# Four edits to the expert stage of an attention, expert and mixing kernel: no branch hints, other places for the half sums, other dealing of the decodes, an earlier turn in the last expert

## The chip, the cores and the metric

The kernel runs on one core of one Trainium2 chip. The metric is device time in microseconds (us) of one launch. Three runs of the kernel before took 632.85 to 635.07 us, with a median of 633.88 us. One further run was recorded by the profiler; it took 635.4 us, and every row below is from it.

A core has five engines that each work through an instruction list of their own: PE (matrix multiplication, with its weight loads shown apart as PEld), DVE (vector), ACT (scalar), POOL and SP. Here SP issues the large loads, and POOL issues gathers, scatters and some writes. Engines wait for each other and for transfers (DMA) by semaphores.

## The reference

Three parts follow each other. The middle one, a mixture of experts with one expert for each token, is the part that matters:

```python
x = attention(q, k, v)                  # 2 x 768 tokens of 512
for b, s in tokens:
    e = argmax(x[b, s] @ w_gate)        # or the expert of the token before, where a gate says so
    p = softmax(x[b, s] @ w_gate)
    h = maximum(x[b, s] @ w1[e], 0)     # 512 -> 1024
    out[b, s] = p[e] * (h @ w2[e])      # 1024 -> 512
# then: FFT over both axes, real part, add, normalise, feed-forward 512 -> 2048 -> 512
```

All operands are float32. The kernel keeps the precision by splitting each operand into a high part and a low rest (names ending in h and l, such as `sl0h` and `sl0l`), and it multiplies three times: high by high, high by low, low by high.

## The kernel before, in words

Attention comes first, with the routing of the tokens beside it. The experts 0 to 7 follow (here e0 to e7), from 118 to 318 us, and then the FFT and the feed-forward part up to 633 us.

The routing sorts tokens by expert into blocks of 128. `expert` (L1262) handles one expert. For experts 1 to 6 two versions of the code stand behind a branch on the number of blocks: `wide` for two blocks or more, `narrow` for one. Every engine takes this branch by itself (`L1348` in the profile is its line). With the data here, e4 and e6 are narrow and the others wide. The branch falls through into `wide`; `narrow` stands behind it in the instruction list. In the kernel before, a hint for PE's branch is given one expert ahead (its instruction has line L1936 in the trace).

The narrow version does this. `first128` (L1232) multiplies the 128 tokens by w1 in two halves `u` of 512 columns. PE forms a half in PSUM; ACT copies it to SBUF as a half sum, `hs[u]` (L1259); PE turns the half sum in four transposes (L1243); ACT applies the maximum and makes the high part `hh` (L1245); DVE makes the low part `hl` (L1246). The second half is turned later, inside `second` (L1197), which multiplies by w2 into `y` (L1204): after five of its 24 matmuls, `late()` issues the transposes of half sum 1. At the end ACT scales `y` into a tile named `ys` (L1186), and POOL scatters it to the output rows (L1191).

While PE works for expert e, ACT and DVE prepare the weights of expert e+1. This is the background, a list of steps that the foreground deals out: `step()` after every third matmul takes two steps, and `drain()` takes all that are left. A weight arrives in units of 1 MB in four raw buffers; SP's load for the unit four places on in a fixed order (`plan`, `shade` L958) is issued when a unit is finished. A unit `e` takes two casts on ACT (`take`, L1048) and two subtractions on DVE (L1050); a unit `d` is a decode for the feed-forward weights: one ACT pass into a tile `dec` (L1081), four DVE passes (L1090 to L1096), and a write of 512 KB by POOL's queue (L1014). Expert e has four `e` units, two in each half of its work, and up to two decodes. `tokens` (L1171) also runs in the background: it turns the next expert's tokens (`turn`, L1158: four transposes on PE, ACT makes `xh`, DVE makes `xl`) and issues the gathers of the expert after that into `xg0`, `xg1`, and a third one for block 2. `place(e, 2)` is that third gather buffer of expert e.

The tile name `dec` has two buffers, the name `ys` two as well. In the kernel before, a narrow expert's half sums stand in a `dec` tile.

The last expert, e7, takes `first128` and `second` for each of two blocks, and a third block (`third`, L1286) between them. `rest` (L1374) is a loop for more blocks that the data here doesn't need; it is a branch that is skipped.

Of the kernel before, what the change touches and what calls it, by code (L numbers as in the profile page):

```python
# [11 lines left out]
F32 = mybir.dt.float32  # L12
# [11 lines left out]
P = 128  # L24
B, H, S, D = 2, 8, 768, 64
E, F = 8, 1024
DM = H * D
# [643 lines left out]
SPLIT = 6  # L671
WARM = 6, 6, 3
TOKENS = 4
CASTS = (5, 6, 7, 8)
RESTS = (24, 25, 26, 27)
AHEAD = dict(enumerate([0, 1, 2, 2, 2, 1, 1, 1, 4, 0, 0, 0, 0, 0, 1, 0, 0, 4, 1, 1, 1, 0, 0, 0, 2, 1, 1, 1], 4))
# [260 lines left out]
class Ring:  # L937
# [20 lines left out]
    @staticmethod  # L958
    def shade():

        d = iter([("d", n) for n in range(2 * EARLY)])
        plan = []
        for e in range(E - 1):
            g = 4 * e + 4
            a = [("e", g), ("e", g + 1)]
            b = [("e", g + 2), ("e", g + 3)]

            for _ in range(-(-min(e + 1, E - 2) * 2 * EARLY // (E - 2)) + -min(e, E - 2) * 2 * EARLY // (E - 2)):
                (a if len(a) == 2 else b).append(next(d))
            plan.append((a, b))  # L970
        plan.append(([("t", 0), ("t", 1)], []))
        return plan
# [127 lines left out]
class Moe:  # L1100
# [158 lines left out]
            A.copy(hs[u], ps)  # L1259
        return lambda: turned(1)  # L1260

    def expert(self, e, n, more, ahead=None):  # L1262
        tc, ring = self.tc, self.st.ring
        pc, ent = self.pc[e % 2], self.ent[e % 4]
        w1, w2 = rows(self.st, 4 * e), rows(self.st, 4 * e + 2)
# [11 lines left out]
        def result(c, h, y, ys, *more):  # L1277
            y = self.second(*h, w2, *y, *more)
            bg.drain()
            last = e == LAST and c == 1  # L1280
            write = lambda: self.write(y, pc[:, c:c + 1], ent[:, c, 1:2], ys, "first" if last else None)
            if last:
                self.finish = write
            else:
                write()

        def third():
            self.weight(e, (2,))

            with tc.If(n > 2):  # L1290
                for _ in self.turn(2, 0, self.place(e, 2)):
                    pass
                if e == LAST:
                    self.rest(more)
                late = self.first128(w1, *self.more, spare, spare)
                result(2, self.more[1], spare, "more", lambda: None, late)

        def pieces():
            for units in ring.plan[e]:
# [23 lines left out]
                    result(at + 1, own(hs, 1), spare, "more")  # L1323

        def narrow():
            first, then = pieces()
            bg.add(chain(*first))
            h = own((self.hh[0], self.hl[0]), 0)
            late = self.first128(w1, own((self.xh[e % 2], self.xl[e % 2]), 0), h, (self.ps_h, "h"), (self.ps_x, "xtp"), step)
            bg.drain()  # L1330
            bg.add(chain(*then))
            calls = iter(range(8))

            def behind():
                if next(calls) == TOKENS:
                    bg.add(self.tokens(e + 1))
                bg.step(2)

            result(0, h, (self.ps_y, "y"), "ys", behind, late)

        if e < LAST:
            if e + 2 < E:
                self.entries(e + 2)
                tc.mark_branch_hint_location(f"wide{e + 1}", hint=(ahead > 1), engines=[mybir.EngineType.PE])
            if e == 0:
                wide()
                return
            with tc.If(n > 1, label=f"wide{e}") as arm:  # L1348
                wide()
            with arm.Else():  # L1350
                narrow()
            return

        for c in range(2):
            x, h = (own(s, c) for s in ((self.xh[e % 2], self.xl[e % 2]), (self.hh[0], self.hl[0])))
            late = self.first128(w1, x, h, (self.ps_h, "h"), (self.ps_x, "xtp"), step, [x[:, :DM] for x in self.xg[:2]])
            if c == 0:
                third()
                bg.add(chain(*first))
            result(c, h, (self.ps_y, "y"), "ys", step, late)  # L1360
            if c == 0:
                self.fetch(0)
# [56 lines left out]
    def run(self):  # L1419
        tc, st = self.tc, self.st  # L1420
        nc = tc.nc
        ring = st.ring
        self.entries(0, (1, 2))
        for x in self.xg[2:]:
            nc.vector.memset(x, 0.0)
        rows = self.gathers(0, (1, 2))
        self.entries(1)
        w = ring.load(2 * PIECES - 2)
        tc.add_manual_dep(w.ins, rows[1].ins.name, mybir.DependencyInfo(mybir.DependencyClass.Sync, mybir.DependencyReason.DATA),
                          reason="this load would hold the rows up")  # L1430
        self.scatter(st.ye, st.ent0[:, 1:2])
        spare = self.ps_more.tile([P, DM], F32, name="more")
        keep_busy(nc, st, spare, WARM[0])
        counts = nc.values_load(st.nch[0:1, E + 1:E + 2], min_val=0, max_val=2 * 4 ** E - 1)
        keep_busy(nc, st, spare, WARM[1])
        for _ in self.tokens(0):
            pass
        keep_busy(nc, st, spare, WARM[2])
        ring.load(2 * PIECES - 1, nc.scalar)
        for e in range(E):  # L1440
            self.expert(e, (counts >> 2 * e) & 3 if e < LAST else counts >> 2 * e, counts >> 2 * E, (counts >> 2 * (e + 1)) & 3 if e + 2 < E else None)


def post(tc, ctx, st):
# [495 lines left out]
```

## Time and profile before

| what | us |
|---|---|
| median of three runs | 633.88 |
| the profiled execution | 635.4 |
| span in it, first to last instruction | 633.6 |
| e2, e3, e5, wide | 23.4, 23.5, 23.6 |
| e4, narrow, 220.6 to 242.3 | 21.7 |
| e6, narrow, 265.9 to 282.4 | 16.5 |
| e7, 282.4 to 318.0 | 35.6 |

[...]

### The profile page before, as it was taken

Reading aid. Unit: us, or ns where it says so; the run is one execution under the profiler, and the core shown is the slowest. Engines: PE = TensorE matmul, PEld = TensorE weight load, DVE = VectorE, ACT = ScalarE, POOL = GpSimd, SP = SyncE. Lnnn points to the kernel's source line nnn. Section 1 sums busy time; section 2 is a strip of 40 time slices with the busy share of each in tenths; the row PEclk is TensorE's granted clock in tenths of the full one; section 3 lists DMA queues with packets and bytes.
Section 4 is the critical chain, followed back from the end, with each engine's and each line's share of the span. In section 5 each row is a group of like instructions: output and inputs, shape, how many; then the busy total and the mean of one; then the engine's idle time right before and its main releaser. Section 6 shows DMA issues by size and latency. Waiting matters only on the chain.

```text
span 633.6 us, 9722 instructions
## 1 busy us (share of the span) xinstructions
PE 609.5 (96%) x3506; PEld 494.1 (78%) x3507; DVE 383.8 (61%) x898; ACT 275.3 (43%) x548; POOL 100.5 (16%) x147
## 2 busy tenths in 40 slices
PE   9999998799999969898999999999999999999997
PEld 4777875499899849687867887888888888888885
DVE  5778786279786968661389987997531221272112
ACT  5789883266475556552434533441121221131010
POOL 2146662315313312300100000000000000000000
PEclk9999999999999989989999999999999999999999
DMA  8568762279978989961260242551100100100001
GB/s 278 187 204 203 201 120 68 49 283 337 372 250 278 335 288 327 339 210 66 87 250 32 95 173 92 187 190 63 67 0 1 32 36 0 67 2 0 1 0 66
DMA packets 25192, 92.49 MB, mean 146 GB/s; under 512 B 7645, under 2 KB 8797, under 8 KB 17185
## 3 DMA queue, kind: packets, MB, share of 16 engines
q1 hardware_dynamic: 19664, 79.50, 37.6%
q0 software_dynamic: 4736, 10.56, 4.6%
q10 hardware_dynamic: 720, 1.55, 0.7%
q8 instruction: 36, 0.59, 0.4%
q14 instruction: 36, 0.29, 0.2%
HBM read 81.00 MB, written 14.84 MB: 151 GB/s over the span
## 4 chain that ended last, share of the span: by engine, by line
PE 52%; DVE 1%; ACT 0%; issue 0%; DVEq 0%; ACTq 0%
PE h L1742 21%; PE acc L1757 7%; PE acc L1756 7%; PE acc L1758 7%; PE y L1204 1%; PE acc L1576 1%; PE acc L1562 1%; PE more L1254 1%; PE h L1254 1%; PE more L1204 1%; PE f L1708 1%; PE f L1605 1%; PE h L50 1%; PE f L1627 0%; DVE u L1767 0%; PE acc L1565 0%
## 5 line engine op out<-in xcount | busy, mean ns | idle before, releaser
L1747 DVE SCALAR_TENSOR_TENSOR hl<-h,hh 128x512 fp32r<-128x512 f32 x48 | 33.1, 689 | 117.5 <-ACT hh L1746 117.5
L1746 ACT ACTIVATE hh<-h 128x512 fp32r<-128x512 f32 x48 | 28.8, 600 | 164.3 <-PE h L1742 164.3
L1050 DVE TENSOR_TENSOR wide<-raws,wide 128x1024 fp32r<-128x1024 f32 (+1 forms) x38 | 44.8, 1201 | 24.4 <-ACT wide L1048 24.4
L168 ACT ACTIVATE t<-t,nm 128x256 f32<-128x256 f32 (+1 forms) x96 | 46.0, 480 | 10.7 <-DVE nm L159 9.9
L1742 PE MATMUL h<-un0h,wide 128*128 128x512 f32 (+1 forms) x136 | 42.4, 378 | 0.1
L1048 ACT CAST wide<-raws 128x1024 fp32r<-128x1024 f32 (+2 forms) x42 | 40.6, 993 | 4.1 <-PE acc L1758 3.4
L159 DVE CUSTOM_DVE_ANT_0 t<-sp,bias 128x256 f32<-128x256 f32 (+1 forms) x96 | 32.8, 398 | 8.3 <-PE sp L150 4.4
L1757 PE MATMUL acc<-wide,hh 128*128 128x512 f32 x96 | 37.8, 393 | 0.0
L1756 PE MATMUL acc<-wide,hh 128*128 128x512 f32 x96 | 37.6, 392 | 0.0
L1758 PE MATMUL acc<-wide,hl 128*128 128x512 f32 x96 | 37.5, 390 | 0.0
L1133 POOL DMA_INDIRECT xg<-xs,ent x23 | 28.7, 1250 | 39.9 <-PE y L1204 17.4
L1742 PEld LDWEIGHTS h<-un0h,wide 128*128 128x128 f32 x136 | 25.0, 188 | 5.0 <-ACT un0h L1517 0.3
L178 PE MATMUL tp<-consts,t 128*128 128x128 f32 x176 | 26.1, 283 | 1.7 <-ACT p L184 1.7
L178 PEld LDWEIGHTS tp<-consts,t 128*128 128x128 f32 x176 | 18.9, 141 | 9.3 <-ACT p L184 4.9
L1742 PE MATMUL h<-un0l,wide 128*128 128x512 f32 (+1 forms) x68 | 25.6, 377 | 0.0
L192 PE MATMUL sm<-p,vs 128*64 128x128 f32 x352 | 24.5, 279 | 0.0
L184 ACT COPY p<-tp 128x512 f32<-128x512 f32 (+1 forms) x48 | 24.3, 537 | 0.3 <-PE tp L178 0.3
L1081 ACT ACTIVATE dec<-raws 128x1024 f32<-128x1024 f32 x18 | 20.6, 1143 | 4.8 <-issue 4.8
L1224 PE MATMUL h<-xh,wide 128*128 128x256 f32 x160 | 22.5, 279 | 0.0
L1096 DVE SCALAR_TENSOR_TENSOR dec<-raws,dec 128x1024 int32<-128x1024 int32 x18 | 22.0, 1225 | 0.6
L1094 DVE SCALAR_TENSOR_TENSOR dec<-raws,dec 128x1024 int32<-128x1024 int32 x18 | 22.0, 1222 | 0.4
L192 PEld LDWEIGHTS sm<-p,vs 128*64 128x64 f32 x352 | 18.7, 136 | 3.8 <-issue 3.8
(474 smaller groups left out, 1602.3 us busy)
## 6 DMA issues: line engine op xcount, KB each, us to landing
raws<-we SPq DMA_DIRECT2D x31, 1024.0 KB
raws<-wm SPq DMA_DIRECT2D x18, 1024.0 KB
raws<-wmf SPq DMA_DIRECT2D x7, 1024.0 KB
wmf<-dec POOLq DMA_DIRECT2D x8, 512.0 KB
xs<-xrow SPq DMA_DIRECT2D x12, 260.0 KB
vs<-v SPq DMA_DIRECT2D x6, 512.0 KB
raws<-kq SPq DMA_DIRECT2D x3, 1024.0 KB
u<-x SPq DMA_DIRECT2D x6, 512.0 KB
```

Of the source, the lines that this page charges most:

```text
L159: V.tensor_tensor_reduce(out=u.t[:, x, :u.W], in0=u.sp[:, j, k, :u.W], in1=bias[:, 4 * u.g + x, u.b0:u.b0 + u.W], scale=-0.125, scalar=3.0 ...
L168: A.activation(u.t[:, x, :u.W], u.t[:, x, :u.W], AF.Exp, bias=u.nm[:, x:x + 1], scale=-1.0, accum_out=u.den[:, x])
L178: T.transpose(u.tp[k][:, j, c], u.t[:, 2 * k + j, c * P:(c + 1) * P], st.ident)
L192: T.matmul(turned[j * D:j * D + D, k], vs[:, ti % KS, u.h + 2 * k + j], u.p[:, 2 * k + j, c], start=c == 0, stop=c == len(tiles) - 1)
L1048: (first or nc.scalar.copy)(hi[:, cs], raw[:, cs])
L1050: (eng() if callable(eng) else eng or nc.vector).tensor_tensor(lo[:, cs], raw[:, cs], hi[:, cs].bitcast(F32), op=ALU.subtract)
L1742: nc.tensor.matmul(ps[:, c], a[:, k], x[:, k, c], start=n == 0, stop=n == 11)
L1746: nc.scalar.activation(hh, ps, AF.Relu)
L1747: nc.vector.scalar_tensor_tensor(hl, ps, 0.0, hh.bitcast(F32), op0=ALU.max, op1=ALU.subtract)
L1756: T.matmul(acc[c], hh[:, cs], h2, start=first, stop=False)
L1757: T.matmul(acc[c], hh[:, cs], l2, start=False, stop=False)
L1758: T.matmul(acc[c], hl[:, cs], h2, start=False, stop=last)
```

## The change

First, the number of decodes beside each expert is given by a tuple (`DECODED`) instead of a formula. The formula gives 2, 1, 1, 2, 1, 1, 0 for e0 to e6; the tuple 2, 1, 2, 2, 0, 1, 0. One decode moves from the first half of e4 to the second half of e2.

Second, the hints to PE's branches go, with the label and the argument that they need.

Third, in `narrow` all units of the expert go into the background in another order (the first two `e` units, then behind `drain` the other two and last the decodes), a step after three matmuls takes one unit of work instead of two, and the half sums stand elsewhere: the first in `place(e, 2)`, the second in a tile of the name `ys`.

Fourth, in the last expert the third block's tokens are turned in the background of the first block (always, not only if there is a third block), and `rest` follows the third block's result.

```diff
+DECODED = 2, 1, 2, 2, 0, 1, 0
...
-            for _ in range(-(-min(e + 1, E - 2) * 2 * EARLY // (E - 2)) + -min(e, E - 2) * 2 * EARLY // (E - 2)):
+            for _ in range(DECODED[e]):
                 (a if len(a) == 2 else b).append(next(d))
...
             with tc.If(n > 2):
-                for _ in self.turn(2, 0, self.place(e, 2)):
-                    pass
+                if e < LAST:
+                    for _ in self.turn(2, 0, self.place(e, 2)):
+                        pass
+                late = self.first128(w1, *self.more, spare, spare)
+                result(2, self.more[1], spare, "more", lambda: None, late)
                 if e == LAST:
                     self.rest(more)
-                late = self.first128(w1, *self.more, spare, spare)
-                result(2, self.more[1], spare, "more", lambda: None, late)
...
         def narrow():
-            first, then = pieces()
-            bg.add(chain(*first))
+            units = [u for part in ring.plan[e] for u in part]
...
+            takes = {u: ring.take(*u) for u in units}
+            d = [takes[u] for u in units if u[0] == "d"]
+            bg.add(chain(*(takes["e", 4 * e + 4 + k] for k in range(2))))
             h = own((self.hh[0], self.hl[0]), 0)
-            late = self.first128(w1, own((self.xh[e % 2], self.xl[e % 2]), 0), h, (self.ps_h, "h"), (self.ps_x, "xtp"), step)
+            late = self.first128(w1, own((self.xh[e % 2], self.xl[e % 2]), 0), h, (self.ps_h, "h"), (self.ps_x, "xtp"), bg.step,
+                                 [self.place(e, 2)[:, :DM], self.work.tile([P, DM], F32, name="ys", bufs=2)])
             bg.drain()
-            bg.add(chain(*then))
+            bg.add(chain(*(takes["e", 4 * e + 6 + k] for k in range(2)), *d))
...
-                bg.step(2)
+                bg.step()
...
-                tc.mark_branch_hint_location(f"wide{e + 1}", hint=(ahead > 1), engines=[mybir.EngineType.PE])
...
+        bg.add(self.turn(2, 0, self.place(e, 2)))
         for c in range(2):
```

On ACT, in the narrow version of e4, the list before is this; `dec` is the half sums' tile in the copies of L1259 and the decode's in L1081, `[waits ...]` names the semaphores (DMAHW are SP's loads, DMASW POOL's transfers).

```order
L1048 CAST wide_106<-raws_63 128x1024 [waits DVE_49]
L1259 COPY dec_8489<-h_8490 128x512 [waits DMASW0_49,DMASW1_49,DVE_49,PE_49]
L1081 ACTIVATE dec_8518<-raws_63 128x1024 [waits DMAHW3_49,DMASW5_49,DVE_49]
L1245 ACTIVATE hh256_6327<-xtp_8525 128x4x128 [waits PE_49]
L1259 COPY dec_8489<-h_8513 128x512 [waits PE_49]
L1048 CAST wide_106<-raws_63 128x1024 [waits DMAHW4_49]
L1245 ACTIVATE hh256_6327<-xtp_8551 128x4x128 [waits PE_49,Activation_49]
L1048 CAST wide_106<-raws_63 128x1024
```

The same place in the changed kernel has the decode no more, and the second half sum in a `ys` tile:

```order
L1260 COPY xg2_6353<-h_8463 128x512 [waits DMASW3_49,PE_49]
L1049 CAST wide_106<-raws_63 128x1024 [waits DMAHW3_49]
L1246 ACTIVATE hh256_6327<-xtp_8490 128x4x128 [waits DVE_49,PE_49,Activation_49]
L1049 CAST wide_106<-raws_63 128x1024
L1260 COPY ys_8462<-h_8481 128x512 [waits DMASW6_49,DMASW7_49,PE_49,Activation_49]
L1049 CAST wide_106<-raws_63 128x1024
L1246 ACTIVATE hh256_6327<-xtp_8515 128x4x128 [waits DVE_49,PE_49]
L1049 CAST wide_106<-raws_63 128x1024
```

The decode of L1081 stood ahead of both `hh` passes and waited for DMASW5, a transfer of POOL; now the second half sum's copy waits for two transfers of POOL, DMASW6 and DMASW7, behind the first `hh` pass.

Which transfers these are is seen on POOL in e3, the expert ahead, here in the changed kernel; the numbers behind a name tell one buffer's use from another.

```order
L1015 DMA wmf_99<-dec_7939 128x1024 [waits DMASW6_49,DVE_49]
L1192 DMA x2_101<-ys_7956,ent3_6335 1536x512 [waits DMASW7_49,Activation_49]
```

POOL issues a decode's write and right behind it the scatter of e3's first block, from a `ys` tile; with two buffers under that name, e4's half sum has the buffer that this scatter reads. The kernel before has the same two instructions in the same order at this place.

On PE, in e7, the third block's turn into the PSUM tile `more` stood behind the branch (L1290) and right ahead of its matmuls:

```order
L1254 MATMUL h_9546<-sl5h_6318,xl1_6349 128x512 x2
L1290 REGISTER_ALU
L1290 COMPARE_AND_BRANCH
L1164 MATMUL more_9579<-consts_66,xg3_6354 128x128 [waits DMASW3_49]
L1164 MATMUL more_9579<-consts_66,xg3_6354 128x128 x3
L1395 REGISTER_ALU
L1395 COMPARE_AND_BRANCH
```

Now it stands three matmuls into the first block:

```order
L1355 UNCONDITIONAL_BRANCH
L1255 MATMUL h_9490<-wide_106,xh1_6346 128x512 [waits PE_49,Activation_49]
L1255 MATMUL h_9490<-wide_106,xh1_6346 128x512 x2
L1165 MATMUL more_9494<-consts_66,xg3_6354 128x128 [waits DMASW3_49]
L1165 MATMUL more_9494<-consts_66,xg3_6354 128x128 x3
L1255 MATMUL h_9490<-wide_106,xh1_6346 128x512
L1255 MATMUL h_9490<-sl5h_6318,xh1_6346 128x512
```

The turn moved ahead of 21 matmuls of the first block, and the branch of `rest` (L1395) behind the third block.

## Rows read from the trace of the kernel before

**Rows 1.** The page's first line

```profile
span 633.6 us, 9722 instructions
```

**Rows 2.** Stretches e2, e3, e4, e6, e7: busy us per engine, PE's clock, DMA share, GB/s

```profile
173.70:197.10 23.40, 23.25 (x153) 21.04 (x152) 16.87 (x21) 13.46 (x17) 5.95 (x7) 1.00 0.83 285
197.10:220.60 23.50, 23.35 (x154) 21.09 (x154) 20.41 (x25) 14.54 (x18) 6.21 (x6) 1.00 0.81 287
220.60:242.30 21.70, 16.24 (x66) 12.57 (x65) 15.14 (x17) 12.70 (x16) 3.75 (x4) 0.84 0.83 294
265.90:282.40 16.50, 14.48 (x64) 11.83 (x65) 10.40 (x10) 11.75 (x15) 1.00 (x1) 0.90 0.63 218
282.40:318.00 35.60, 34.00 (x162) 27.65 (x161) 10.34 (x18) 12.74 (x20) 2.94 (x3) 1.00 0.31 114
```

**Rows 3.** PE's waits, 118 to 330 us: total us, times, longest

```profile
PE y L1204 <- ACT hh L1245: 4.3, 1, 4.3
PE h L1254 <- ACT wide L1048: 2.0, 1, 2.0
PE more L1254 <- DVEq L1395: 1.6, 1, 1.6
```

**Rows 4.** Timeline of e4: start, us, engine, line, operation, [idle before <-releaser]

```profile
221.12 0.59 POOL L1014 DMA_DIRECT2D wmf<-dec  x1 [0.68 <-DVE dec L1096]
...
222.01 1.03 POOL L1191 DMA_INDIRECT x<-ys,ent  x1 [0.30 <-issue]
...
225.47 0.58 ACT L1259 COPY dec<-h 128x512 f32<-128x512 f32 x1
226.10 0.66 PE L1243 MATMUL xtp<-consts,dec 128*128 128x128 f32 x4 [1.16 <-ACT dec L1259]
...
230.80 1.12 ACT L1081 ACTIVATE dec<-raws 128x1024 f32<-128x1024 f32 x1 [4.75 <-issue]
231.81 0.59 ACT L1245 ACTIVATE hh<-xtp 128x512 fp32r<-128x512 f32 x1
232.45 0.79 PE L1204 MATMUL y<-sl0h,hh 128*128 128x512 f32 x1 [4.30 <-ACT hh L1245]
232.75 1.07 ACT L1048 CAST wide<-raws 128x1024 fp32r<-128x1024 f32 x1
233.28 0.68 DVE L1246 SCALAR_TENSOR_TENSOR hl<-xtp,hh 128x512 fp32r<-128x512 f32 x1
234.75 1.05 PE L1243 MATMUL xtp<-consts,dec 128*128 128x128 f32 x4
236.27 1.22 DVE L1050 TENSOR_TENSOR wide<-raws,wide 128x1024 fp32r<-128x1024 f32 x1
```

**Rows 5.** Shorter stretches, columns as in rows 2

```profile
222.00:232.00 10.00, 4.99 (x23) 3.48 (x21) 4.69 (x5) 5.25 (x7) 2.58 (x2) 0.99 0.98 354
...
232.40:238.60 6.20, 6.15 (x17) 4.88 (x18) 6.13 (x8) 4.12 (x6) 0.58 (x1) 0.50 0.46 136
...
267.90:272.80 4.90, 4.88 (x15) 3.86 (x16) 4.63 (x4) 3.36 (x4) 0.05 (x1) 0.65 0.79 254
```

**Rows 6.** PE's branches into e4 (216 to 220 us): ns min/median/max, first and last start

```profile
L1348 PEldq COMPARE_BRANCH  x2: 196/272/349, 216.5 to 217.3; - x2
```

**Rows 7.** The same into e6, 261 to 263 us

```profile
L1348 PEldq COMPARE_BRANCH  x2: 302/2913/5524, 261.7 to 262.2; - x2
```

**Rows 8.** PE's hints, all six

```profile
L1936 PEldq BRANCH_PREFETCH_HINT  x6: 32/36/39, 126.2 to 239.4; - x6
```

**Rows 9.** Timeline: PE's first matmul of e6

```profile
267.92 0.47 PE L1254 MATMUL h<-sl0h,xh 128*128 128x512 f32 x1 [2.03 <-ACT wide L1048]
```

**Rows 10.** Timeline of the third block's start in e7

```profile
288.47 0.60 PE L1164 MATMUL more<-consts,xg 128*128 128x128 f32 x4
...
289.78 0.69 DVE L1168 TENSOR_TENSOR xl<-more,xh 128x512 fp32r<-128x512 f32 x1 [1.07 <-ACTq L1395]
...
290.67 1.16 PE L1254 MATMUL more<-wide,xh 128*128 128x512 f32 x4 [1.60 <-DVEq L1395]
```

More of the change, by code (lines that the diff above doesn't have):

```diff
@@ L1260, in first128, with expert @@
         return lambda: turned(1)
-    def expert(self, e, n, more, ahead=None):
+    def expert(self, e, n, more):
         tc, ring = self.tc, self.st.ring
@@ L1325, in narrow @@
         def narrow():
-            first, then = pieces()
-            bg.add(chain(*first))
+            units = [u for part in ring.plan[e] for u in part]
+            for u in units:
+                if u[0] == "d":
+                    ring.begun.pop(ring.at[u], None)
+            takes = {u: ring.take(*u) for u in units}
+            d = [takes[u] for u in units if u[0] == "d"]
+            bg.add(chain(*(takes["e", 4 * e + 4 + k] for k in range(2))))
             h = own((self.hh[0], self.hl[0]), 0)
-            late = self.first128(w1, own((self.xh[e % 2], self.xl[e % 2]), 0), h, (self.ps_h, "h"), (self.ps_x, "xtp"), step)
+            late = self.first128(w1, own((self.xh[e % 2], self.xl[e % 2]), 0), h, (self.ps_h, "h"), (self.ps_x, "xtp"), bg.step,
+                                 [self.place(e, 2)[:, :DM], self.work.tile([P, DM], F32, name="ys", bufs=2)])
             bg.drain()
-            bg.add(chain(*then))
+            bg.add(chain(*(takes["e", 4 * e + 6 + k] for k in range(2)), *d))
             calls = iter(range(8))
@@ L1347, in expert @@
                 return
-            with tc.If(n > 1, label=f"wide{e}") as arm:
+            with tc.If(n > 1) as arm:
                 wide()
@@ L1440, in run @@
         for e in range(E):
-            self.expert(e, (counts >> 2 * e) & 3 if e < LAST else counts >> 2 * e, counts >> 2 * E, (counts >> 2 * (e + 1)) & 3 if e + 2 < E else None)
+            self.expert(e, (counts >> 2 * e) & 3 if e < LAST else counts >> 2 * e, counts >> 2 * E)
 def post(tc, ctx, st):
```

## The prediction

> **What bounds the kernel.** I read the page's first line, then the table by stretches, then the list of PE's waits, and last the timeline at each wait. PE sets the time nearly everywhere: in e2 and e3 it is busy for all but 0.15 us of 23.4 and 23.5 us [rows 2]. So an edit pays only where PE stands still, or runs at the lower clock. Between 118 and 330 us three waits are long: 4.3 us ahead of `y` in e4, 2.0 us ahead of e6, 1.6 us in e7's third block [rows 3]. e4 has 16.24 us of work in 21.7 us, at a mean clock of 0.84; e6 14.48 in 16.5, e7 34.00 in 35.6 [rows 2]. The change touches all three places.
>
> The timeline tells why e4 waits. POOL issued e3's decode write at 221.12 and a scatter behind it at 222.01. The decode of ACT (L1081), whose `dec` buffer that write reads, began at 230.80 after 4.75 us of idling put down to "issue", that is, to nothing that the profile shows. Behind it on ACT stood the first `hh` (231.81), and `y` could start only at 232.45 [rows 4]. So I take it that 512 KB took about 9.7 us to leave, in a stretch in which the DMA engines were 0.98 busy [rows 5]. After this, PE had the clock at 0.50 until 238.6 [rows 5].
>
> **e4, the decode goes.** Without it the first `hh` follows its transposes at once, and the 4.3 us wait as it is now vanishes. What is late next is the second half sum. Its copy stands in a `ys` tile and waits for two transfers of POOL; the order shows that they are e3's decode write and the scatter behind it, which reads the same buffer. Their landing has no row. The write's end is bounded by the decode's start, 230.80; the scatter was issued 0.89 us later (222.01 less 221.12), so it lands between 230.8 and 231.7, and I take 231.2, in the middle. The cover of the old wait is gone only in part: a wait on the same queue comes back, one half sum later, but with the first half of the work done before it.
>
> From there the chain is worked out. The copy takes 0.58, so it ends at 231.8. The next on ACT is a cast of 1.07, to 232.9. DVE then has four subtractions of the 1.22 kind, one `hl` of 0.68 and two `xl` of 0.69 [rows 4, 10]: 4.88 + 0.68 + 1.38 = 6.94, to 239.8. e5 uses its `xl` only after eight of its matmuls, about 1.0 us: e2's 23.25 us hold 96 matmuls of 256 columns and 48 of twice the width [rows 2], so a narrow one takes 23.25 / 192 = 0.12. So e5 starts as if at 238.8. PE's own chain is shorter: from the late transposes at 234.75 to e5 at 242.30 it took 7.55 us, 3.85 of it at half clock [rows 2, 4, 5], so about 5.6 at the full clock and 7.5 at worst, which gives 237.4 to 239.4 from 231.8. I take 238.7. Against 242.3 [rows 2] that is a gain of 3.6 us. With the landing 2 us later it is 1.6; with no wait on it at all, what PE, ACT and DVE have to do is left, and the gain is about 5.5.
>
> **e4, no hint.** The trace holds six hints and both outcomes: the branch into e4 took 0.349 us, the one into e6 5.524 us [rows 6, 7], and both had a hint about one expert earlier [rows 8]. Without one I cost e4's branch like e6's: between 0.35 and 5.52, and I take 5.52. It starts at 217.3 [rows 6], so PE enters e4 at 222.8 instead of 220.6, 2.2 us late. 24 matmuls of 0.24 follow and four transposes of 0.66 [rows 4], 6.4 us at full clock, to 229.2, and five of `y` to 230.4; the wait of 1.16 for the first half sum's copy at 225.47 [rows 4] may go or stay, since fewer casts are ahead of it. That is ahead of the half sum at 231.8, so the landing hides the stall. If the clock falls as it did behind e6's stall (0.65 of full over 4.9 us, a loss of 1.7 us [rows 5]), PE is there at 232.1, about level. So the term is 0 here; uncovered it is 2.2 to 3.9 us.
>
> [...]
>
> **e6.** Its wait of 2.03 us is put down to ACT's cast [rows 9], but the sequencer's branch of 5.524 us from 262.2 ends at 267.7, and PE starts at 267.92 [rows 7, 9]; I take the branch for the cause. A hint that did nothing there is removed, so the stall stays, and so do the 1.7 us of clock [rows 5]. The background now goes at half the pace, one step instead of two, and what is left comes behind `drain`; ACT is busy 11.75 of 16.5 us and DVE 10.40 [rows 2], so there is room. One side is a loss of 3.3 us, a second such wait inside e6's code, of which PE's queue covers a little less than of the first (5.52 less 2.03, 3.5 us); the other a gain of 1, should casts no longer stand ahead of `hh`. I take a loss of 0.5 for a cast of 1.07 that now stands between a half sum and its `hh` about half of the time.
>
> **e7.** The third block's turn was issued at 288.47, its `xl` at 289.78, and the matmuls that need it began at 290.67 after 1.60 us [rows 10]. Now the turn stands among the first block's matmuls, some 5 us earlier, and its ACT and DVE passes lie beside those. The four transposes of 0.60 stay on PE. The gather was long in place, since the turn at 288.47 waited for none. Late next would be the branch of `rest`, but it is now behind the third block, where PE has queued matmuls. Gain 1.6, bounds 0 and 1.7.
>
> **e2.** A second decode costs ACT 1.12 us [rows 4] and DVE about 3.5, the difference between e3, which has two already (20.41), and e2 with one (16.87); and e3 has no PE wait [rows 2]. The transfer grows by 1.5 MB, about 3.9 us at the 390 GB/s or so that e3's and e4's busiest stretches come to (354 in [rows 5], at a share of 0.98, would make it 4.2). e2 has 0.17 of 23.4 us free, 4.0 us [rows 2]. That just fits; if not, e3's weights come late and PE waits. Bounds 0 and 1.5 us; I take 0.2, near e3's row. Nothing is won there.
>
> **Sum.** 3.6 + 1.6 - 0.5 - 0.2 = 4.5 us. The profiled execution took 635.4 us, 1.8 beyond its span [rows 1], so 630.9; it lies 1.5 above the median of 633.88, and on the median this is 629.4 us. The FFT and the feed-forward part are PE-bound, and I cost them at nothing.
>
> **Rivals.** (A) The forecast, 627.6 to 631.2 us, chance 0.53.
>
> (B) A far branch without hint is not covered: a stall of 2.2 us and its 1.7 us of clock in e4, or the second such wait of 3.3 us in e6. For it: the e6 row, and new places of the code. Against: the landing at 231.2 covers e4. It takes 3.3 from the gain: 632.7. Chance 0.15: one branch in two stalls, but e4's is covered. [...]
>
> (C) e2's extra 1.5 MB doesn't fit, and e3's casts are late by 2 us: 631.4. For it: 3.9 against 4.0 us free. Against: e3 has two decodes at a share of 0.81. Chance 0.11.
>
> (D) The half sum's copy isn't held, since the scatter lands by 229: the e4 term is 5.5 instead of 3.6, which gives 627.5. For it: one transfer fewer is queued in e4. Against: the decode of before did wait until 230.80 [rows 4]. Chance 0.09.
>
> (E) Slower. The scatter behind e3's decode write lands much later, since with no decode in e4 its loads follow each other closer and take the DMA engines from POOL's queue, which were 0.98 busy already [rows 5]. ACT then stands at the half sum's copy, with every cast and `hh` of e4 behind it, and PE waits. Each us beyond 231.2 costs one: nothing is left at 231.2 + 4.5 = 235.7, and from 237.6 the kernel is slower by over 1.9. With a landing at 238 the time is 636.2. Against: the loads in flight are four of 1 MB in either kernel. Chance 0.12.
>
> **Numbers.** What a measurement here can tell from no change is about 0.3%, 1.9 us, so faster is below 632.0 and slower above 635.8. Faster: A, C, D but for their upper tails, 0.71. Same: B and these tails, 0.17. Slower: E, 0.12. The range leaves out most of E and half of the far tails: 627.0 to 633.0 us; its upper end holds B.
>
> **What would show it.** In the profile after, PE's wait ahead of the late transposes (L1244) in e4 should be named, 1 to 2 us, with ACT's half sum copy ending near 231.8 and idle ahead of it; e5's first matmul near 238.7; a branch of about 5.5 us into e4 and into e6; the third block's matmuls in e7 without a wait; e2 and e3 of 23.4 to 23.6 us. A copy that ends past 236, a second branch wait inside e6, or PE waiting in e3 for a cast would make the prediction wrong.

## The result, and the profile after

The changed kernel is slower: 639.73 us in the median of 20 runs against 635.26 us of the kernel before, ratio 1.0077 (95% interval 1.0061 to 1.0094). The forecast was 629.4 us and faster. It was worked out from a median of 633.88 us for the kernel before, so 1.4 of the 10.3 us between forecast and measurement are in that starting point. The profiled execution has a span of 638.2 us against 633.6 [rows 1].

The stages are measured from PE's first matmul of one expert to the first of the next, so a wait ahead of an expert counts for the one before it. The table holds the kernels that the text argues with; times are us.

| kernel | e0 | e3 | e4 | e5 | e6 | e7 |
|---|---|---|---|---|---|---|
| before | 23.1 | 23.4 | 21.7 | 25.6 | 14.5 | 38.6 |
| changed | 24.5 | 27.8 | 15.5 | 25.9 | 18.9 | 37.6 |
| changed, second profile (`again`) | 23.2 | 31.7 | 14.7 | 25.8 | 18.1 | 37.5 |
| dealing alone (`only1`) | 23.2 | 23.4 | 14.3 | 26.2 | 14.5 | 38.6 |
| dealing, decodes last in `narrow` (`dlast`) | 23.2 | 25.5 | 20.5 | 26.1 | 14.5 | 38.6 |
| changed, units in the plan's order (`inplan`) | 23.1 | 25.5 | 14.5 | 26.1 | 18.5 | 37.5 |
| changed, code moved (`pad`) | 23.2 | 28.0 | 14.3 | 28.3 | 14.5 | 37.5 |
| dealing and last expert, code moved (`only14s`) | 23.1 | 25.0 | 13.0 | 24.1 | 14.3 | 37.7 |

e4 gained 6.2 us and e7 1.0; e3 lost 4.4 and e6 4.4. In this execution e0 also began 1.4 us later than in the kernel before and took 1.3 us more; the run `again` below shows that these two belong to the one execution. PE's waits in the changed kernel, from 118 to 330 us (total us, times, longest), name the places; they answer to [rows 3]:

```profile
PE h L1255 <- issue: 5.7, 2, 3.7
...
PE h L1225 <- DVE hl L1229: 1.9, 1, 1.9
...
PE h L1255 <- ACT more L1187: 1.2, 1, 1.2
PE xtp L1244 <- ACT ys L1260: 1.0, 1, 1.0
PE xtp L1244 <- ACT xg L1260: 0.9, 1, 0.9
...
PE y L1205 <- PEq L1403: 0.6, 1, 0.6
```

The 4.3 us of e4 and the 1.6 us of e7 are gone, as forecast. New are 1.9 us in e3 for `hl`, and 5.7 us "issue" ahead of the narrow code: 2.0 at e4 and 3.7 inside e6. The stretches e2, e3, e4, e6 and e7 (columns as in [rows 2], the bounds being first matmuls):

```profile
176.40:199.82 23.42, 23.27 (x154) 21.06 (x153) 20.11 (x25) 14.49 (x18) 5.89 (x6) 1.00 0.80 276
199.82:227.63 27.81, 23.78 (x153) 21.04 (x152) 21.05 (x26) 15.10 (x19) 8.48 (x10) 1.00 0.90 323
227.63:243.09 15.46, 13.56 (x65) 10.32 (x65) 9.82 (x10) 10.90 (x14) 1.98 (x2) 1.00 0.85 291
...
269.01:287.89 18.88, 15.19 (x64) 12.19 (x65) 9.76 (x10) 10.68 (x14) 0.86 (x1) 0.82 0.51 167
287.89:325.48 37.59, 36.80 (x173) 29.52 (x171) 13.40 (x26) 13.58 (x23) 3.03 (x3) 1.00 0.38 138
```

e2 with its second decode is as long as before, at a DMA share of 0.80. The trouble begins in e3. Its timeline in the changed kernel (ACT, DVE, PE):

```profile
200.06 0.69 ACT L1187 ACTIVATE more<-more,pc 128x512 f32<-128x512 f32 x1 [4.80 <-PE more L1205]
...
204.53 1.05 ACT L1049 CAST wide<-raws 128x1024 fp32r<-128x1024 f32 x1 [3.77 <-DMA raws<-wm]
...
205.48 0.59 ACT L1228 ACTIVATE hh<-h 128x512 fp32r<-128x512 f32 x1
...
206.75 0.68 DVE L1229 SCALAR_TENSOR_TENSOR hl<-h,hh 128x512 fp32r<-128x512 f32 x1
...
207.49 0.39 PE L1225 MATMUL h<-xh,sl0h 128*128 128x256 f32 x1 [1.91 <-DVE hl L1229]
```

ACT stands 3.77 us at a cast of an expert's unit, and what releases it is a load of `wm`, the feed-forward weights, which this cast doesn't read. Behind it on ACT stands `hh`, behind that on DVE `hl`, and PE waits 1.91 us. The same in e4 (ACT and PE):

```profile
230.45 2.00 ACT L1049 CAST wide<-raws 128x1024 fp32r<-128x1024 f32 x2 [4.01 <-DMA raws<-we]
...
232.35 0.58 ACT L1260 COPY xg<-h 128x512 f32<-128x512 f32 x1
...
232.98 0.66 PE L1244 MATMUL xtp<-consts,xg 128*128 128x128 f32 x4 [0.92 <-ACT xg L1260]
...
236.52 0.59 ACT L1260 COPY ys<-h 128x512 f32<-128x512 f32 x1 [1.21 <-DMA wmf<-dec]
...
237.16 0.66 PE L1244 MATMUL xtp<-consts,ys 128*128 128x128 f32 x4 [0.98 <-ACT ys L1260]
```

Here the first casts wait 4.01 us with the first half sum's copy behind them. The last two rows are the wait that the prediction had named: the `ys` copy, for e3's decode write.

PE's branches into e4 and into e6 in the changed kernel (ns min/median/max, first and last start):

```profile
L1355 PEldq COMPARE_BRANCH  x2: 174/2884/5594, 221.4 to 221.9; - x2
```

```profile
L1355 PEldq COMPARE_BRANCH  x2: 281/2496/4712, 263.6 to 264.1; - x2
```

The first is 5.594 us where [rows 6] has 0.349. And e6 stops a second time, three matmuls and four weight loads in (PE's timeline):

```profile
269.01 0.47 PE L1255 MATMUL h<-sl0h,xh 128*128 128x512 f32 x1 [1.20 <-ACT more L1187]
269.32 0.39 PE L1255 MATMUL h<-sl0l,xh 128*128 128x512 f32 x1
269.55 0.40 PE L1255 MATMUL h<-sl0h,xh 128*128 128x512 f32 x1
273.64 0.58 PE L1255 MATMUL h<-sl0l,xh 128*128 128x512 f32 x1 [3.69 <-issue]
```

What PE's sequencer waits for is in the trace too. The view of DMA transfers has queues of the kind "instruction"; one of them, q8, moves packets of 16 KB (0.02 MB). In the straight code from 329.4 to 597.9 us of the kernel before it moved ten of them while PE ran 1255 matmuls and 1254 weight loads, 251 recorded instructions a packet. Within the branch into e4, from 221.9 to 227.5 us:

```profile
q8 instruction: 1, 0.02, 1.0%
```

The second stop of e6, from 269.9 to 273.6 us, holds one too; the branch of [rows 6] holds none. In the sixteen profiles of this text, all 23 branches into e4 and e6 that took 4.5 us or more hold such a packet, the nine of about 0.35 us hold none, and the sequencer goes on 1.3 to 1.5 us after the packet has ended. Behind a slow branch, then, and in the second stop, PE waits for instructions.

PE ran at the lower clock from 271.4 to 278.2 us, granted 0.50 of full speed, twice as long as behind the one stall ahead of e6 before (0.65 over 4.9 us is 3.4 us at half [rows 5]).

### The profile page after: what moved, and what is told of

It is laid out like the page before. It is cut to its first block, busy times and chain, and to the rows that moved or that the text cites. A ratio compares the mean times of both kernels' runs of the same rounds, so it can differ in the third digit from the quotient of the medians.

```text
span 638.2 us, 9698 instructions
## 1 busy us (share of the span) xinstructions
PE 609.3 (95%) x3506; PEld 493.5 (77%) x3507; DVE 383.6 (60%) x898; ACT 275.0 (43%) x548; POOL 101.1 (16%) x147
## 3 DMA queue, kind: packets, MB, share of 16 engines
q1 hardware_dynamic: 19664, 79.50, 37.6%
## 4 chain that ended last, share of the span: by engine, by line
PE 50%; DVE 1%; ACT 0%; issue 0%; DVEq 0%; ACTq 0%
PE h L1750 21%; PE acc L1765 7%; PE acc L1764 7%; PE acc L1766 7%; PE y L1205 1%; PE acc L1584 1%; PE acc L1570 1%; PE h L1255 1%; PE f L1716 1%; PE f L1613 1%; PE h L50 1%; PE f L1635 0%; DVE u L1775 0%; PE acc L1573 0%; PE f L1616 0%; PE acc L1635 0%
## 5 line engine op out<-in xcount | busy, mean ns | idle before, releaser
L1764 PE MATMUL acc<-wide,hh 128*128 128x512 f32 x96 | 37.6, 392 | 0.0
L1766 PE MATMUL acc<-wide,hl 128*128 128x512 f32 x96 | 37.5, 390 | 0.0
L178 PE MATMUL tp<-consts,t 128*128 128x128 f32 x176 | 26.1, 283 | 1.7 <-ACT p L184 1.2
L178 PEld LDWEIGHTS tp<-consts,t 128*128 128x128 f32 x176 | 18.9, 140 | 9.3 <-ACT p L184 4.2
L1750 PE MATMUL h<-un0l,wide 128*128 128x512 f32 (+1 forms) x68 | 25.6, 377 | 0.0
L192 PE MATMUL sm<-p,vs 128*64 128x128 f32 x352 | 24.5, 280 | 0.0
L1750 PE MATMUL h<-un1h,wide 128*128 128x512 f32 x64 | 21.3, 396 | 0.0
```

The source lines that it names most:

```text
L178: T.transpose(u.tp[k][:, j, c], u.t[:, 2 * k + j, c * P:(c + 1) * P], st.ident)
L192: T.matmul(turned[j * D:j * D + D, k], vs[:, ti % KS, u.h + 2 * k + j], u.p[:, 2 * k + j, c], start=c == 0, stop=c == len(tiles) - 1)
L1750: nc.tensor.matmul(ps[:, c], a[:, k], x[:, k, c], start=n == 0, stop=n == 11)
L1764: T.matmul(acc[c], hh[:, cs], h2, start=first, stop=False)
L1766: T.matmul(acc[c], hl[:, cs], h2, start=False, stop=last)
```

## The experiments

The medians of the kernel before lie between 633.0 and 635.3 us in the separate jobs, so each run is given by its ratio to the kernel before in the same job. Two kernels are compared by their ratios. Code is said to move by places: one place is one entry of PE's instruction list, and the matmuls used for it take two each, one for the weight load and one for the matmul.

**Code moved by matmuls that never run (`pad`).** In the arm for general attention, which this data doesn't take:

```diff
     with arm.Else():
+        with tc.tile_pool(name="ps_pad", bufs=1, space=PSUM) as ps:
+            keep_busy(nc, st, ps.tile([P, 512], F32, name="busy"), 7)
         general_attention(tc, st, io, Route(tc, st, io))
```

> The changed kernel, with 7 matmuls put into the arm of the first branch that is not taken with this data (the general attention): they are never executed and only move all of PE's later instructions by 21 places. Theory 1 (place of the code): after the change e6's narrow code starts about 7 PE instructions ahead of the end of a block of instructions that is fetched as one, so PE waits a second time for a fetch (3.7 us) and then runs at half clock; moved by 21 places the second wait goes, e6 takes 14.5 to 15 us instead of 18.9, and the time falls by 4 to 4.5 us, to about 635.3, level with the kernel before. Theory 2 (the hints themselves), theory 3 (the dealing of the decodes) and theory 4 (the half sums' buffers): nothing changes, 639.7, ratio 1.007.

The seven matmuls take 14 places, not the 21 of the expectation; that puts e6's narrow code where it stands in the kernel before. Measured: 1.0033 (1.0016 to 1.0051). e6 is 14.5 us and its second stop is gone. Its branch took 7.1 us in this profile and made e5 2.4 us longer, so the kernel gains 0.44%, 2.8 us, of the 4.4 us. The place of the code makes the second stop, and it is about half of what the change lost.

**Hints back (`hints`).** The hints (six in the trace) are put back, with the label and the argument that they need.

> The changed kernel with the six hints put back; this moves PE's later instructions by 24 places too. Theory 1 (place of the code): e6 is mended as in the run with idle matmuls in the arm not taken, about 635.3. Theory 2 (the hints): beside that the branch into e4 takes 0.35 instead of 5.59 us and PE's 2.0 us of waiting ahead of e4 go, 633.3 or less; if theory 1 is wrong and only the hints count, 637.7 with e6 still at 18.9 us. Theory 3 (the dealing): 639.7.

Measured: 0.9998 (0.9976 to 1.0021). e6 is 14.5 us, the branch into e4 takes 0.341 us. Still there are 1.9 us for `hl` in e3, and 3.3 us in e4 for the first half sum's copy; the profile is of the longest of twelve executions (637.52 us, the median is 633.72), so these sizes may be above the usual ones. So hints and place together explain the distance to the kernel before, and neither explains why nothing is won.

**The old dealing (`deal`).** `DECODED = 2, 1, 1, 2, 1, 1, 0` in the changed kernel.

> The changed kernel with the decodes dealt 2, 1, 1, 2, 1, 1, 0 as before. Theory 3 (the decode moved to e2 makes e3's weights late): PE's 1.9 us wait for hl in e3 goes, and e4 gets its decode back; behind the half sums it should cost PE at most 1 us there, so 637.8 to 638.8. Theory 1 (place of the code): e6 stays at 18.9 us with its second fetch wait, so not below 637. If the decode out of e4 is what gained there, e4 goes from 15.5 back to near 20 us, and the time is 641 or more.

Measured: 1.0143 (1.0112 to 1.0174). The changed kernel loses with the old dealing too, and more. The time is in the range that was expected if e4 went back to 20 us, but it is not lost there: e4 takes 14.4 us, and e5 takes 33.7 us, where PE waits for `hl` up to 3.9 us:

```profile
PE h L1225 <- DVE hl L1229: 4.6, 2, 3.9
```

**The kernel before, with its code moved by 81 matmuls (`shift`).** As `pad`, with 81 matmuls, to bring e6's narrow code to the place within a packet of instructions that it has in the changed kernel. I counted three places for a matmul, 243 in all.

> [...] Theory 1 (place of the code): the kernel before gets the second fetch wait in e6, 3 to 3.7 us and a longer half clock, 639 to 639.8, ratio 1.006 to 1.007. Theories 2 to 4: nothing changes, 635.3, ratio 1.000.

Measured: 0.9988 (0.9971 to 1.0005): no loss. But the run does not test the second stop as it was meant to. A matmul takes two places (the trace of the kernel before has 64 of these matmuls on L50 and 64 weight loads), so 81 are 162 places and not 243, and e6's narrow code did not come to that place. What the run shows is that the two narrow versions changed roles. The branch into e4:

```profile
L1348 PEldq COMPARE_BRANCH  x2: 307/2452/4597, 216.9 to 217.9; - x2
```

and the one into e6:

```profile
L1348 PEldq COMPARE_BRANCH  x2: 194/270/347, 261.0 to 261.4; - x2
```

Now e4 stalls, where the decode's wait hides it, and e6 doesn't: PE has no wait ahead of e6 any more, which bears out the prediction's reading that the branch, and not ACT's cast, was the cause of that wait. With the hints in place, the place of the code decides which of the two branches is slow. Whether a hinted branch can have a second stop is not shown: no hinted kernel here has e6's code at the place that it has in the changed kernel.

**The decode in e6 (`later`).** The kernel of `hints` with `DECODED = 2, 1, 1, 2, 0, 1, 1`.

> The changed kernel with the hints back and the moved decode dealt to e6 instead of e2: 2, 1, 1, 2, 0, 1, 1. Theory A (the loads: with two decodes in e2 a load of e3's stretch comes late, its cast on ACT stands ahead of hh, PE waits 1.9 us and then runs at half clock): e3 goes from 27.2 us with the hints back to 23.5, so 629 to 630.5 beside 633.0 for the kernel before; e6 may lengthen by 1 to 2 us, since its DVE has 12 us of work in 14.4 and gets 3.7 more. Theory B (only the places of the code and the hints count): as with the hints alone, ratio 1.000, 633.

Measured: 0.9958 (0.9943 to 0.9973). Better by 0.4%, as theory A had it in the number, but e4 keeps 3.0 us of waiting for the first half sum, and 1.0 us for `hl` is in e2 now. The waits aren't tied to the decode in e2.

**The dealing alone (`only1`).** The kernel before with the tuple:

```diff
+DECODED = 2, 1, 2, 2, 0, 1, 0
...
+            for _ in range(DECODED[e]):
```

> The kernel before with the new dealing of the decodes alone (2, 1, 2, 2, 0, 1, 0). Theory A (the loads): e3 gets its wait for hl and takes 27 us instead of 23.4, and e4 loses the decode that stood ahead of hh: 21.7 to about 17 to 18; in sum between 1 us faster and 1 us slower, ratio 0.998 to 1.002. Theory B: e4 gains 4 us, e3 is as before, ratio 0.993 to 0.995.

Measured: 0.9908 (0.9887 to 0.9929), 627.61 us. Theory A is refuted: e3 has no wait at all, so the loads come in time with two decodes in e2 and in e3. And e4 takes 14.3 us, 7.4 less than before, more than theory B had. ACT's first cast in e3 (timeline):

```profile
197.53 1.04 ACT L1049 CAST wide<-raws 128x1024 fp32r<-128x1024 f32 x1
```

It begins 0.8 us after e3's first matmul (196.70), without a wait; in the changed kernel, under the same dealing, it begins 4.7 us after it (204.53 less 199.82).

**Without the hints alone (`only2`).** The kernel before with the hint lines removed.

> The kernel before without the six hints and nothing else. Theory B (the hints and the places of the code): the branch into e4 takes 5.5 us instead of 0.35, and PE enters e4 2 us late; whether that shows depends on the decode's wait behind it (4.3 us), which hides it. e6's code moves 24 places to another place in its block of instructions, so a second fetch wait there is possible or not. 633 if all is hidden, 637 with a second wait in e6. Theory A: no change, 633.

Measured: 1.0029 (1.0012 to 1.0047). The branches into e4 and e6 take 5.9 and 4.8 us, and e6 is 17.3 us with a second stop of 2.55 us:

```profile
269.90 0.63 PE L1254 MATMUL h<-sl0h,xl 128*128 128x512 f32 x2 [2.55 <-DVE sl5l L1050]
```

The profile names a DVE subtraction here, but this matmul doesn't read what that one writes. e6's code stands 10 PE instructions ahead of where the changed kernel has it, and the stop comes behind eight matmuls instead of three: five matmuls and their five weight loads later. In `inplan` below, 4 places ahead, it comes behind five:

```profile
268.40 0.58 PE L1255 MATMUL h<-sl1l,xh 128*128 128x512 f32 x1 [3.30 <-issue]
```

So in these three kernels the stop stands at a fixed place of the instruction list, not at a wait of the program. In e4 the stall costs nothing: the decode's wait of 4.3 us is gone from PE's list, the half clock lasts 3.4 us instead of 6.8, and e3 and e4 take 41.3 us together against 45.1.

**The narrow version and the last expert alone (`only34`).** The kernel before with these two parts, hints and old dealing kept.

> The kernel before with the new narrow version and the new last expert, but with the hints and the old dealing (2, 1, 1, 2, 1, 1, 0). Theory A: e3 is 23.4 us, but e4 now starts its decode behind all its casts, so that the decode's buffer and the loads behind it come late to e5, as in the changed kernel with the old dealing, where e4 and e5 took 48.1 us together against 47.4 before; e7 gains 1.0: 633 to 636, and no second fetch wait in e6. Theory B: 631.

Measured: 1.0057 (1.0033 to 1.0080), 0.1% over the expectation of 633 to 636. e4 and e5 take 52.1 us together against 47.3 before, in a profiled execution of 639.51 us, 2.8 above the median. These parts lose by themselves. With the new dealing that leaves one suspect, what `narrow` does to the other experts.

That is seen in the order of the instructions. In e2 SP issues its loads, in the wide version of the changed kernel:

```
L987 DMA raws_63<-we 128x2048 [waits DMAHW4_49,DVE_49]
L991 DMA raws_63<-wm 128x2048 [waits DMAHW5_49,DMAHW7_49,DMAHW2_49,DVE_49]
L987 DMA raws_63<-we 128x2048 [waits DMAHW6_49,DVE_49,Activation_49]
L987 DMA raws_63<-we 128x2048 [waits DVE_49,Activation_49]
L991 DMA raws_63<-wm 128x2048 [waits DMAHW1_49,DVE_49]
L987 DMA raws_63<-we 128x2048 [waits DMAHW2_49,DVE_49,Activation_49]
```

and in the narrow one, which is not taken there:

```
L987 DMA raws_63<-we 128x2048 [waits DMAHW4_49,DVE_49]
L991 DMA raws_63<-wm 128x2048 [waits DMAHW5_49,DMAHW7_49,DMAHW2_49,DVE_49]
L987 DMA raws_63<-we 128x2048 [waits DMAHW6_49,DVE_49]
L991 DMA raws_63<-wm 128x2048 [waits DMAHW1_49,DVE_49]
L987 DMA raws_63<-we 128x2048 [waits DVE_49,Activation_49]
L987 DMA raws_63<-we 128x2048 [waits DMAHW2_49,DVE_49,Activation_49]
```

The expert's own units stand in another order: the third load of the wide list is the fifth of the narrow one, and the fifth of the wide list is a `wm` load. Loads take SP's semaphores (DMAHW1, 2, 3 and so on) in the order in which they are issued, so the same unit has DMAHW3 in the wide version and DMAHW5 in the narrow one. What reads it behind the branch can't know which version ran, and waits for both; and in the wide version, which ran, DMAHW5 is that of the later `wm` load. ACT's first cast in e3, in the kernel of `only1` and then in the changed one:

```
L1049 CAST wide_106<-raws_63 128x1024 [waits DMAHW3_49]
L1049 CAST wide_106<-raws_63 128x1024 [waits DMAHW5_49,DMAHW3_49]
```

**The decodes last in `narrow`, and nothing else (`dlast`).** The kernel of `only1` with:

```diff
             first, then = pieces()
+            kinds = [[u[0] for u in units] for units in ring.plan[e]]
+            d = [t for ts, ks in zip((first, then), kinds) for t, k in zip(ts, ks) if k == "d"]
+            first, then = ([t for t in ts if t not in d] for ts in (first, then))
+            then += d
             bg.add(chain(*first))
```

> The kernel before with the new dealing, as in the run of the dealing alone, and in the narrow version the decodes put behind the e units. The narrow versions that run with this data (e4 and e6) have no decode under this dealing, so what is executed is the same; only the instructions of the narrow versions that are not taken (e1, e2, e3, e5) stand in another order. Theory J (join): behind the branch, a cast waits for the load that filled its raw buffer in either version; where the two versions issue their loads in another order, it waits for two loads, one of them not its own (in the order list, casts that wait for two of SP's transfers go from 3 to 11), so e3 gets its wait for hl again, 2 to 4 us, e4's first casts come late, and the time is 631 to 634. Theory A (transfers really late by the dealt decode) and theory B (hints, place of the code): as with the dealing alone, 627.6, ratio 0.991.

Measured: 1.0048 (1.0026 to 1.0069), 1.4% over `only1`, though SP, ACT and DVE execute the same instructions in the same order in both traces; only what they wait for differs. The place of PE's code is no rival here: it moved by two places, and both branches took as long as in `only1` (0.344 us into e4, 5.564 into e6). The loss is larger than theory J had it (631 to 634 us; 636.87 measured). ACT's timeline has both waits of the changed kernel, at the head of e3 and of e4:

```profile
201.87 1.05 ACT L1049 CAST wide<-raws 128x1024 fp32r<-128x1024 f32 x1 [3.61 <-DMA raws<-wm]
...
227.84 3.88 ACT L1049 CAST wide<-raws 128x1024 fp32r<-128x1024 f32 x4 [4.07 <-DMA raws<-we]
```

PE waits behind them, 5.1 us of it in e4 and 1.8 in e3:

```profile
PE xtp L1244 <- ACT dec L1260: 6.4, 2, 5.1
...
PE h L1225 <- DVE hl L1229: 1.8, 1, 1.8
```

e4 goes from 14.3 to 20.5 us, part of it at half clock (a mean of 0.83). This settles the cause of the waits in e3 and e4: the order of loads in a version that is not taken.

**The units in the plan's order, in the changed kernel (`inplanh` with the hints, `inplan` without).**

```diff
-            bg.add(chain(*(takes["e", 4 * e + 4 + k] for k in range(2))))
+            bg.add(chain(*(takes[u] for u in ring.plan[e][0])))
...
-            bg.add(chain(*(takes["e", 4 * e + 6 + k] for k in range(2)), *d))
+            bg.add(chain(*(takes[u] for u in ring.plan[e][1])))
```

> The changed kernel with the hints back and with the narrow version's units taken in the order of the plan (the decodes where they stand there, no more at the end); half sums, one step after three matmuls and the last expert as changed. What e4 and e6 execute is the same as with the hints alone (633.0 on the scale of the kernel before). Theory J (join): the double waits go, e3 takes 23.4 us and e4's casts start right away: 626.5 to 628, ratio 0.988 to 0.992. Theory A: 633, ratio 1.000.

> The changed kernel, without hints, with the narrow version's units in the order of the plan. Theory J: e3 without its wait; but the branches into e4 and e6 cost PE 2 to 3 us each, and e6's code starts 4 places ahead of where it is in the changed kernel, so the second fetch wait stays: 632 to 635, some 5 us under the changed kernel. Theory A: as the changed kernel, 639.

Measured: `inplanh` 0.9944 (0.9920 to 0.9968) against 0.9998 of `hints`; `inplan` 1.0006 (0.9985 to 1.0026) against 1.0077 of the changed kernel, inside its expectation. The waits for `hl` in e3 and for the first half sum are gone in both. `inplanh` misses its expectation by 0.2%. In its profile the hinted branch into e4 took 7.5 us all the same, and PE stood 4.4 us; but that is the longest of its eleven executions (634.42 us, the median is 630.13), and whether the others had this wait is not on record. In `inplan` the forecast wait of the second half sum stands alone (ACT):

```profile
231.11 0.59 ACT L1260 COPY ys<-h 128x512 f32<-128x512 f32 x1 [1.52 <-DMA x<-ys,ent]
```

**The dealing and the last expert (`only14`).** `only1` with the diff's lines in `third` and in the last expert.

> The kernel before with the new dealing and the new last expert, and nothing else. If the turn ahead is worth what the stages of the changed kernel show (e7 38.8 to 37.8 us), this is 1.0 us under the dealing alone: 626.6, ratio 0.989. If e7's gain is an accident of the code's place, 627.6.

Measured: 0.9898 (0.9864 to 0.9931), 627.58 us. The profile has e7 at 37.6 instead of 38.6 us, but the intervals of the two kernels overlap: the run does not tell 1.0 us from nothing.

**Once more, the changed kernel (`again`).**

> The changed kernel, once more. If the late start and the half clock in e0 belong to it, e0 again starts at 128.5 us and takes 24 us; the time is 1.007 to 1.008 of the kernel before. If they belong to one execution, e0 starts between 126.6 and 127.9 and takes 23, as in the other kernels without hints, and the span is about 635.5, while e3 (27 to 28 us), e4 (15.5) and e6 (18.8) are as in the first profile.

Measured: 1.0094 (1.0068 to 1.0119). e0 starts at 127.5 us and takes 23.2, so the late start and the half clock in e0 were those of one execution. The span is 637.8 all the same, and not the 635.5 expected then: the wait for `hl` was 2.6 us and e4's stall 4.0, and e3 came to 31.7 us.

```profile
PE h L1255 <- issue: 7.6, 2, 4.0
PE h L1225 <- DVE hl L1229: 2.6, 1, 2.6
```

**The best, with its code moved by 81 matmuls (`only14s`).** `only14` with the 81 matmuls of `shift` (again 162 places, not 243).

> The kernel before with the new dealing and the new last expert, with all of PE's later instructions moved by 243 places (81 matmuls in the arm that is not taken). Theory of the code's place: as in the kernel before moved by 243, the branch into e6 takes 0.35 instead of 5.7 us, so PE's wait of 2.2 us ahead of e6 goes and there is no half clock behind it, up to 3.5 us less in e5 and e6; the branch into e4 takes 4.6 us instead of 0.35, and now no decode's wait hides it, so e3 to e4 loses 2 to 2.5 us. In sum 625.5 to 628, ratio 0.986 to 0.990 (only14: 0.990). If the place doesn't decide, both branches are as in only14, 627.6.

Measured: 0.9882 (0.9857 to 0.9907), 625.81 us, the fastest kernel here, though its interval overlaps those of `only14` and `only1`. The branches changed roles as in `shift` (4.521 us into e4, 0.342 into e6), and the clock is 1.00 from e3 to e6:

```profile
197.45:222.44 24.99, 23.44 (x153) 20.91 (x152) 20.85 (x26) 15.70 (x20) 8.63 (x9) 1.00 0.98 352
222.44:235.42 12.98, 12.98 (x64) 10.66 (x65) 10.43 (x10) 10.47 (x14) 2.43 (x2) 1.00 0.96 358
235.42:259.49 24.07, 23.65 (x153) 21.23 (x152) 18.31 (x26) 13.45 (x17) 10.46 (x9) 1.00 0.89 309
259.49:273.75 14.26, 13.13 (x66) 10.49 (x64) 10.44 (x10) 11.64 (x15) 1.05 (x2) 1.00 0.74 259
```

## Why the prediction was wrong

- **The step that failed: costing the new order in `narrow` by the two experts that run it.** I took `narrow` to act in e4 and e6 alone. Its order of loads also decides, at the end of each branch, what the next expert's casts wait for, in experts whose narrow version never runs. No term and no rival had it; a wait in e3 could only have come from the e2 term, which was costed at 0.2 us for the transfers alone. It cost 0.7% by `inplan` against the changed kernel (0.71%, 4.5 us; 0.88%, 5.6 us, with the ratio of `again`), and 1.4% where the rest was the old narrow version. The sign was there to be read ahead: casts behind the branch that name two of SP's semaphores instead of one.
- **e6: the right mechanism as a rival, the wrong size in the sum.** I took a loss of 0.5 us and gave a second branch wait 3.3 us as a part of (B), at 0.15. It came: 3.69 us of waiting and a longer half clock, e6 at 18.9 and 18.1 us. For the 0.5 us of the term, the runs have 18.9 - 14.5 = 4.4 us in the stage against `pad`, and 2.8 us in the kernel's time.
- **e4 without its hint.** The branch was 5.594 us as costed, the wait 1.97 for 2.2. That the half sum hides it held in part at best: in `inplan` e3 and e4 take 40.0 us together, in `only1`, where the branch takes 0.352 us, 37.7. The traces have 0.34 to 0.35 us and no packet of instructions for some placements, and 4.5 to 7.6 us and a packet for others. What makes a placement slow is not shown.
- **e4 without its decode: right in mechanism and nearly in time.** The wait moved to the `ys` copy, which ended at 231.7 in `inplan` (231.11 plus 0.59) for 231.8 forecast, and PE's wait there was 1.2 us (0.98 in the changed kernel). From e4's first matmul to e5's it took 15.5 us; the forecast had 238.7 less 222.8, 15.9. The term of 3.6 us was too small all the same: e3 and e4 together go from 45.1 us to 40.0 in `inplan`, 5.1 less, and to 37.7 in `only1`. The dealing alone is worth 0.92% (5.8 us) of the kernel's time. What `inplan` lacks against `only1` in these two experts is mostly the branch into e4, for which PE waits 1.9 us; e4 itself takes 14.3 us with the old half sums (`only1`) and 14.5 with the new ones (`inplan`), so their new place gained nothing.
- **e7.** The wait of 1.6 us went; 0.6 us came back as PE's wait for the branch of `rest` (L1403), so 1.0 us is left in the stage, and only14 doesn't resolve it.
- **e2.** Right: its length is unchanged, and in `only1` e3 has no wait. The 390 GB/s of the term is what the kernel before moved from 213 to 217 us, in e3.
- **Rivals.** (C) is refuted by `only1`, and (E), as the scatter's landing, by `inplan`; (D) didn't occur. (B) came true in e6.
- **The signs.** All three that the prediction named came. The second branch wait inside e6 is (B)'s. PE waited in e3 behind a cast, but for the join and not for the transfers of (C). The copy of the half sum ended at 237.1 us, past 236, but not by (E): POOL issued the decode's write at 226.67 us, 5.6 later than before, because e3 began late and ran late, and the copy began 9.85 us after it, where the prediction had read 9.7.

The terms put in order: the forecast's -4.5, plus 4.5 for the join, plus 3.9 for e6 (4.4 less the 0.5 counted), plus 0.6 for e7, is +4.5 us; measured was 0.77% of 635.26, +4.9 us. That this closes so well is in part luck: with the 2.8 us that `pad` gives e6 in the kernel's time it would be +2.9, and the e4 term was itself too small by 1.5 us.

Open: why the hinted branch into e4 was slow in the profile of `inplanh`. In `dlast` and `hints`, where e4's code starts 3 places before and 3 places behind that of `inplanh`, it took 0.34 us, so the place alone doesn't tell; two packets of instructions came within that branch instead of one. Open too is how much of what `only1` is ahead of `inplanh` is that branch's wait, and how much the half sums' place or the single step.

## What to carry to other kernels

A branch has two sides, and what is written in the side that isn't taken can set waits for what stands behind the join (1.4% in `dlast`): let both sides issue the transfers that outlive them in the same order, and compare the semaphores that the first readers behind the join name. Change one thing at a time where several gain in different places: here the dealing alone was 0.9% faster and the whole 0.8% slower. Where code is branched to, adding or removing a few instructions anywhere ahead moves it, and a difference of nearly half a per cent (0.44% in `pad`) can come from the place alone; instructions in an arm that is not taken tell that apart. And a profile is one execution: look where its time lies among the others before a wait in it is taken for the kernel's.

## What the runs showed of the hardware that was not expected

- A jump to narrow code cost PE's sequencer 0.34 to 0.35 us or 4.5 to 7.6 us, with nothing in between in these runs; the long ones, and only they, hold a 16 KB packet of instructions. With the hint, moving the code by 81 matmuls (162 places) exchanged the two cases between e4 and e6.
- Behind an unhinted jump a second wait of 3.69 us came after three matmuls, in a stretch of straight code, with another such packet; with the code 4 and 10 places ahead it was 3.30 us after five and 2.55 us after eight.
- PE's clock fell to half in e6 in twelve of the sixteen profiles and stayed there for 3.4 or 6.8 us; in `only1` it did so behind a wait of 2.1 us, in `only14` behind 2.2 us at the same place it didn't, and in `only14s`, without a wait at that place, it was at 1.00 throughout the experts.
- Two profiles of the same kernel differed by up to 4 us in e3 and by 1.3 us in e0, in opposite directions, at spans of 638.2 and 637.8 us.
